# One ring tile and one ScalarE eviction a tick for O^T and dQ^T in a two-block attention backward

## The chip, the cores and the metric

The kernel runs on one core of one Trainium2 chip. The metric is the device time of one execution in microseconds (us). Engines: TensorE (PE) multiplies, PEld is its weight load, VectorE (DVE), ScalarE (ACT) and GpSimd (POOL) do the rest of the arithmetic, and SyncE (SP) issues DMAs. TensorE writes to PSUM, which has eight banks. SBUF holds everything else.

## The reference: what is computed

Two independent blocks, A and B, each an attention with cached keys and values and its full backward pass. The output of the forward pass and ten gradients are returned, in bf16.

```
B, Sq, D = 8, 96, 640
H, Sk, Dh = 32, 512, 128
q = (x @ wq).reshape(B, Sq, H, Dh).transpose(0, 2, 1, 3)
scores = einsum("bhqd,bhkd->bhqk", q, k_cache) * (Dh ** -0.5)
p = softmax(scores, axis=-1)
o = einsum("bhqk,bhkd->bhqd", p, v_cache)
out = o.transpose(0, 2, 1, 3).reshape(B, Sq, H * Dh) @ wo
...
out0 = concatenate([out_A, out_B], axis=-1)
grads = vjp of all ten inputs at grad_out
```

For one head and batch element (96 query rows, 512 keys) the backward needs dV = P^T dO, dP = dO V^T, dS = P * (dP - delta) with delta the row sums of O * dO, dK = dS^T Q and dQ = dS K. Then dwo = O^T g and dwq = x^T dQ per head, and dx = dQ wq^T summed over the heads. The factor Dh ** -0.5 belongs once to Q (and through it to dK) and once to dQ.

## The kernel before

Work is cut into **ticks**: one tick for each pair of head and batch element, 32 x 8 for each block, 512 in all. The kernel writes its steps into a list (`Emitter`) with a tick and a slot; the list is sorted and run, and a tile scheduler then orders instructions on each engine and inserts the waits. One pair's work is spread over several ticks (`OFF`): S and softmax at +3 (`c_s2a`, `c_s2b`, `c_s3a`, `c_s3b`), P^T and dV at +4, O^T at +5, dP and dS at +6, dS^T and dK at +7, dQ^T at +8. So one tick works on six pairs at different stages.

Within a tick TensorE does, in this order: S; if needed the transposes of K (`c_s1`); dQ^T and the four transposes of dS (`c_s78`, lines 412 and 419); dK (436); O^T and the four transposes of P (`c_s45`, lines 342 and 349); dV (366); dP (394) and delta (396); then work of whole heads: transposes of wo and wq (`pB`), projections of Q and dO (`pC`), natural-order copies (`pD`, `qA`), dwo (`qB`), dwq (`qD`), and the group sums for out and dx (`gU`, line 515).

All results leave PSUM through the 8 banks of one pool (`bank`). Two tiles a tick matter here:

- `optp_ps` (line 332): O^T of one pair in the first 96 fp32 columns, P^T of another behind it. ScalarE evicts both, L352 into `OT_h`, L355 into `PT_sb`.
- `dq_dst_ps` (line 404): dQ^T of one pair in the first 96 fp32 columns, dS^T of another behind it. DVE copies dS^T to `dST_sb` (L421), and ScalarE evicts dQ^T into `dQT_h` with the factor `scale` (L425).

ScalarE otherwise carries the exponential (L307), the evictions of dV (L369) and dK (L439), and some of the heads' evictions (`evac`, L155). DVE carries the row maximum (L297), the reciprocal (L317), dS (L398), copies and sums. POOL scales P (L326), forms `prod` = O^T * dO^T for delta (L384) and issues the stores. The DMA queue of SP brings K and V, and transposes V always and K in half of the ticks.

`OT_h` and `dQT_h` are tiles of one head each, [128, 768] bf16, eight buffers each, from the pool `hst` (lines 218 and 219). They are read by `prod` (OT_h), by the transposes of `qA` (L459) and by `gU`, which adds up to six heads at a time. `gU` evicts the first group to fp32 accumulators, adds later ones on DVE (L517), and writes the last with L535 and L537.

Of the kernel before, what the change touches and what calls it, by code (L numbers as in the profile page):

```python
# [15 lines left out]
class Emitter:  # L16
# [4 lines left out]
    def add(self, tick, slot, fn):  # L21
        self.items.append((tick, slot, self.n, fn))
        self.n += 1
# [21 lines left out]
OFF = dict(ldk=-5, ldv=-3, kt=-3, vt=0, s2=3, s3=3, s4=4, s5=5, s6=6, s7=7, s8=8)  # L45
# [8 lines left out]
def build_block(tc, em, tick0, blk, x, kc, vc, wq, wo, g_all, out_all, dx, dk, dv, dwq, dwo, ident, ones, pools, HG=6, first=True, groups=None):  # L54
    nc = tc.nc
# [3 lines left out]
    T = B * Sq  # L59
# [38 lines left out]
    def bank(shape, dt, name):  # L98
        return ps.tile(shape, dt, name=name, tag="bank")
# [3 lines left out]
    SB = {}  # L103
    HS = pools["HS"]
    CS = pools["CS"]

    stp = pools["stp"]

# [94 lines left out]
    def pB(h):  # L203
        def f():
            st = HS[(blk, h)]
            woT_ps = bank([128, DC * 128], BF16, "woT_ps")
            for c in range(DC):
                nc.tensor.transpose(woT_ps[:, c * 128:(c + 1) * 128], st["wo_h"][:, c * 128:(c + 1) * 128], ident[:])
            woT_h = hd.tile([128, DC * 128], BF16, name="woT_h", bufs=1)
            evac(EV["pB0"], woT_h[:], woT_ps[:])  # L210
            st["woT_h"] = woT_h
            wqT_ps = bank([128, DC * 128], BF16, "wqT_ps")
            for c in range(DC):
                nc.tensor.transpose(wqT_ps[:, c * 128:(c + 1) * 128], st["wq_h"][:, c, :], ident[:])
            wqT_h = hst.tile([128, D], BF16, name="wqT_h")
            evac(EV["pB1"], wqT_h[:], wqT_ps[:])
            st["wqT_h"] = wqT_h
            st["OT_h"] = hst.tile([128, T], BF16, name="OT_h")
            st["dQT_h"] = hst.tile([128, T], BF16, name="dQT_h")
            st["QT_h"] = hd.tile([128, T], BF16, name="QT_h")  # L220
            st["dOT_h"] = hd.tile([128, T], BF16, name="dOT_h")
        return f
# [104 lines left out]
                st["P_sb"] = P_sb  # L327
        return f

    def c_s45(k5, k4, k6):  # L330
        def f():
            pt_ps = bank([128, 1024], BF16, "optp_ps")
            ot_view = None
            if False:
                pass
            if k5 is not None:
                st = CS[(k5[0], k5[1], k5[2])]
                hs = HS[(k5[0], k5[1])]
                tok = slice(k5[2] * Sq, (k5[2] + 1) * Sq)
# [3 lines left out]
                ot_view = (OT_ps, hs, tok)  # L343
            if k4 is not None:
                st4 = CS[(k4[0], k4[1], k4[2])]
                P_sb = st4["P_sb"]
                PT_ps = pt_ps[:, 256:256 + KC * Sq]
                for c in range(KC):
                    nc.tensor.transpose(PT_ps[:, c * Sq:(c + 1) * Sq], P_sb[:, c * 128:(c + 1) * 128], ident[0:Sq, 0:Sq])  # L349
            if ot_view is not None:  # L350
                OT_ps, hs, tok = ot_view
                nc.scalar.activation(hs["OT_h"][:, tok], OT_ps, ACT.Identity, scale=1.0)  # L352
            if k4 is not None:
                PT_sb = wk.tile([128, KC * Sq], BF16, name="PT_sb", bufs=3)
                nc.scalar.activation(PT_sb[:], PT_ps, ACT.Identity, scale=1.0)  # L355
                st4["PT_sb"] = PT_sb
        return f
# [30 lines left out]
    def c_s6(h, b):  # L388
        def f():
# [7 lines left out]
            dS_sb = wk.tile([Sq, Sk], BF16, name="dS_sb", bufs=3)  # L397
            nc.vector.scalar_tensor_tensor(dS_sb[:], dP_ps[:], dl_ps[:, 0:1], st["P_sb"][:], op0=ALU.subtract, op1=ALU.mult)  # L398
            st["dS_sb"] = dS_sb
        return f  # L400

    def c_s78(k8, k7):
        def f():
            x_ps = bank([128, 1024], BF16, "dq_dst_ps")
            dq_view = None
            if k8 is not None:
                st = CS[(k8[0], k8[1], k8[2])]
                hs = HS[(k8[0], k8[1])]
                tok = slice(k8[2] * Sq, (k8[2] + 1) * Sq)
                dQT_ps = x_ps[:, 0:2 * Sq].bitcast(F32)  # L410
                for c in range(KC):
                    nc.tensor.matmul(dQT_ps, st["K_sb"][:, c, :], st["dST_sb"][:, c * Sq:(c + 1) * Sq], start=(c == 0), stop=(c == KC - 1))  # L412
                dq_view = (dQT_ps, hs, tok)
            if k7 is not None:
                st7 = CS[(k7[0], k7[1], k7[2])]
                dS_sb = st7["dS_sb"]
                dST_ps = x_ps[:, 256:256 + KC * Sq]
                for c in range(KC):
                    nc.tensor.transpose(dST_ps[:, c * Sq:(c + 1) * Sq], dS_sb[:, c * 128:(c + 1) * 128], ident[0:Sq, 0:Sq])  # L419
                dST_sb = wk.tile([128, KC * Sq], BF16, name="dST_sb", bufs=3)  # L420
                nc.vector.tensor_copy(dST_sb[:], dST_ps)  # L421
                st7["dST_sb"] = dST_sb
            if dq_view is not None:
                dQT_ps, hs, tok = dq_view
                nc.scalar.activation(hs["dQT_h"][:, tok], dQT_ps, ACT.Identity, scale=scale)  # L425
                del CS[(k8[0], k8[1], k8[2])]
        return f

    def c_s7(h, b):
# [51 lines left out]
    def qD(h, c_lo, c_hi):  # L481
        def f():
# [8 lines left out]
            for ci in range(ncn):  # L491
                c = c_lo + ci
                for t in range(TT):
                    nc.tensor.matmul(w_ps[:, ci * 256:(ci + 1) * 256], S["x_nat"][:, t, c * 128:(c + 1) * 128], dQnat[:, t].rearrange("p a d -> p (a d)"),  # L494
                                     start=(t == 0), stop=(t == TT - 1))
            evac(EV["qD"], dwq_sb[:, c_lo:c_hi, :].rearrange("p a b -> p (a b)"), w_ps[:, 0:ncn * 256])
            st["dwq_n"] += ncn
            if st["dwq_n"] == DC:
                with nc.allow_non_contiguous_dma(reason="dwq slice of two heads"):
# [5 lines left out]
    def gU(g, which, t, gi):  # L505
        def f():
            acc = S.get("out_acc" if which == 0 else "dx_acc")
            dst_flat = out_flat if which == 0 else dx_flat
            (c0, w) = gsplits[gi]
            o_ps = bank([128, w], F32, "o_ps")  # L510
            for hh in range(groups[g]):
# [3 lines left out]
                nc.tensor.matmul(o_ps[:], src[:, t * 128:(t + 1) * 128], rhs, start=(hh == 0), stop=(hh == groups[g] - 1))  # L515
            if 0 < g < NG - 1:
                nc.vector.tensor_tensor(acc[:, t, c0:c0 + w], o_ps[:], acc[:, t, c0:c0 + w], op=ALU.add)  # L517
                return
            if g == 0 and NG > 1:
                evac(EV["gU"], acc[:, t, c0:c0 + w], o_ps[:])  # L520
                return
            end = not first and which == 1
            if end:
# [3 lines left out]
                    S["ob"] = stp.tile([128, D], BF16, name="ob", tag="stage")  # L527
                ob = S["ob"][:]
            if NG == 1:
                evac(EV["gU"], ob[:, c0:c0 + w], o_ps[:])  # L530
            else:
                if end and t in (0, 2):
                    tmp = S["xT"][:].rearrange("p c k -> p (c k)").bitcast(F32)[:, (t // 2) * D + c0:(t // 2) * D + c0 + w]
                    nc.scalar.activation(tmp, o_ps[:], ACT.Identity, scale=1.0)
                    nc.gpsimd.tensor_tensor(ob[:, c0:c0 + w], tmp, acc[:, t, c0:c0 + w], op=ALU.add)  # L535
                else:
                    nc.vector.tensor_tensor(ob[:, c0:c0 + w], o_ps[:], acc[:, t, c0:c0 + w], op=ALU.add)  # L537
# [6 lines left out]
    def k_on_pe(h, b):  # L544
        return (b // NB) % 2 == 0

    S45 = pools["S45"]
    S78 = pools["S78"]
    for g in range(NG):
        h0 = GH0[g]  # L550
        for hh in range(groups[g]):
# [12 lines left out]
            for b in range(B):  # L564
# [18 lines left out]
                S45.setdefault(ct + OFF["s5"], [None, None, None])[0] = (blk, h, b)  # L583
                S45.setdefault(ct + OFF["s4"], [None, None, None])[1] = (blk, h, b)
                S45.setdefault(ct + OFF["s6"], [None, None, None])[2] = (blk, h, b)
                S78.setdefault(ct + OFF["s8"], [None, None])[0] = (blk, h, b)
                S78.setdefault(ct + OFF["s7"], [None, None])[1] = (blk, h, b)
# [26 lines left out]
    pools["c_s78"] = c_s78  # L614
    return tick0 + H * B


def _kernel_impl(tc, A_x, A_k_cache, A_v_cache, A_wq, A_wo, B_x, B_k_cache, B_v_cache, B_wq, B_wo, grad_out,
# [13 lines left out]
    with ExitStack() as ctx:  # L632
# [21 lines left out]
        pools["S45"] = {}  # L654
        pools["S78"] = {}
        pools["HS"] = {}
        pools["CS"] = {}
        em = Emitter()
# [1 line left out]
        for blk, args in enumerate(((A_x, A_k_cache, A_v_cache, A_wq, A_wo, grad_out, out_0, out_1, out_2, out_3, out_4, out_5),  # L660
# [7 lines left out]
        for tk, (k5, k4, k6) in pools["S45"].items():  # L668
            em.add(tk, SLOTS["S5"], pools["c_s45"](k5, k4, k6))
        for tk, (k8, k7) in pools["S78"].items():  # L670
            em.add(tk, SLOTS["S8"], pools["c_s78"](k8, k7))
        em.run()


# [62 lines left out]
```

## Time and profile before

| | |
|---|---|
| Median of 4 runs | 1736.52 us (1720.19 to 1747.04) |
| Profiled execution | 1734.96 us |
| Span of its trace | 1733.2 us, granted TensorE clock 0.997 |
| Busy share PE, PEld | 97%, 78% |
| Busy share ACT, DVE, POOL | 81%, 77%, 61% |
| Instructions on ACT, DVE, POOL | 4027, 3040, 1747 |
| DMA | 424.69 MB, mean 245 GB/s |

A row of instruction groups reads: line, engine, operation, output<-inputs, shapes and count, then total busy us and mean ns of one, then the engine's idle time just before them and what ended it. A row of waits reads: engine and what it wanted to do, what it waited for, total us, number of times, longest us. A row of the chain reads: start in us, length in us, what. The chain is followed back from the last instruction of the program to what released each step. A busy time includes an instruction's tail, in which the next one is already under way.

### The profile page before, as it was taken

To read this page: it belongs to the slowest core of one execution; us is meant where nothing else is said; L and a number is where in the kernel's file an instruction comes from. 1 tells how busy PE (TensorE), PEld (TensorE's weight loads), DVE (VectorE), ACT (ScalarE), POOL (GpSimd) and SP (SyncE) were. 2 spreads that over 40 slices of the span, in tenths; PEclk is the share of its full clock that TensorE was granted. 3 is DMA by queue.
4 is the path that set the end of the run, shared out by engine and by line. 5 is a ranking of instruction groups with operands and counts; after the bars stand their busy time and mean duration, and the time that the engine had idled before them with its cause. 6 is when DMAs were issued, how large, how long until landed. Compare 5 with 4: busy or idle time off the path is not lost.

```text
span 1733.2 us, 57521 instructions
## 1 busy us (share of the span) xinstructions
PE 1681.3 (97%) x21811; PEld 1346.0 (78%) x21976; DVE 1328.5 (77%) x3040; ACT 1411.6 (81%) x4027; POOL 1049.6 (61%) x1747
## 2 busy tenths in 40 slices
PE   8999999999999999999897999999999999999998
PEld 7877778878778777778676777887788778778876
DVE  6876678778878877778776876787788778777877
ACT  7988789779779878878766997997799779868974
POOL 4666466556657656656555764665566557646654
PEclk9999999999999999999998999999999999999999
DMA  9999999989999989999999999999999999989983
GB/s 276 268 247 269 239 238 270 256 214 249 264 208 256 279 202 227 263 253 262 267 235 208 267 275 240 243 266 246 221 251 284 228 214 263 267 216 245 271 223 131
DMA packets 606774, 424.69 MB, mean 245 GB/s; under 512 B 425696, under 2 KB 564320, under 8 KB 606496
## 3 DMA queue, kind: packets, MB, share of 16 engines
q1 hardware_dynamic: 552912, 243.65, 70.7%
q0 software_dynamic: 53584, 177.35, 31.7%
q8 instruction: 172, 2.82, 0.7%
q14 instruction: 106, 0.87, 0.2%
HBM read 161.09 MB, written 159.12 MB: 185 GB/s over the span
## 4 chain that ended last, share of the span: by engine, by line
PE 82%; ACT 8%; DMA 4%; issue 3%; DVE 2%; POOL 1%; SPq 0%; ACTq 0%; DVEq 0%; POOLq 0%
PE o_ps L515 11%; PE q_ps L240 11%; PE S_ps L295 6%; PE dwq_ps L494 6%; PE dK_ps L436 5%; PE dP_ps L394 5%; PE dwo_ps L474 5%; PE dV_ps L366 5%; PE dq_dst_ps L419 4%; PE dq_dst_ps L412 4%; PE optp_ps L349 4%; PE optp_ps L342 4%; ACT E_sb L307 3%; PE n_ps L255 3%; PE kT_ps L282 3%
## 5 line engine op out<-in xcount | busy, mean ns | idle before, releaser
L326 POOL TENSOR_SCALAR P_sb<-E_sb,rinv 96x512 bf16<-96x512 bf16 x512 | 353.4, 690 | 387.0 <-DVE rinv L317 377.6
L307 ACT ACTIVATE E_sb<-S_ps,negm 96x512 bf16<-96x512 f32 x512 | 355.5, 694 | 206.2 <-DVE negm L297 181.5
L398 DVE SCALAR_TENSOR_TENSOR dS_sb<-dP_ps,dl_ps,P_sb 96x512 bf16<-96x512 f32 x512 | 382.8, 748 | 73.9 <-PE dl_ps L396 54.7
L297 DVE TENSOR_REDUCE negm<-S_ps 96x1 f32<-96x512 f32 x512 | 348.1, 680 | 62.5 <-PE S_ps L295 58.1
L439 ACT ACTIVATE dK_sb<-dK_ps 128x512 bf16<-128x512 f32 x512 | 308.5, 603 | 64.2 <-PE dK_ps L436 60.6
L369 ACT ACTIVATE dV_sb<-dV_ps 128x512 bf16<-128x512 f32 x512 | 319.9, 625 | 0.0
L375 POOL DMA_DIRECT2D out_dram<-dV_sb x256 | 194.1, 758 | 148.2 <-ACT dV_sb L369 129.0
L355 ACT ACTIVATE PT_sb<-optp_ps 128x384 bf16<-128x384 bf16 x512 | 261.2, 510 | 1.1 <-PE optp_ps L349 1.1
L375 POOL DMA_DIRECT2D out_dram<-dK_sb x256 | 193.0, 754 | 84.0 <-ACT dK_sb L439 48.7
L394 PE MATMUL dP_ps<-VT,dOT_h 128*96 128x512 bf16 x512 | 195.3, 381 | 10.4 <-DMA VT<-V_sb 9.5
L366 PE MATMUL dV_ps<-dOnat_h,P_sb 96*128 96x128 bf16 x2048 | 198.1, 219 | 1.0 <-DVE dOnat_h L158 0.8
L436 PE MATMUL dK_ps<-Qnat_h,dS_sb 96*128 96x128 bf16 x2048 | 198.1, 219 | 0.0
L384 POOL TENSOR_TENSOR prod<-OT_h,dOT_h 128x96 bf16<-128x96 bf16 x512 | 186.9, 365 | 8.6 <-ACT OT_h L352 4.3
L421 DVE COPY dST_sb<-dq_dst_ps 128x384 bf16<-128x384 bf16 x512 | 177.4, 346 | 11.7 <-PE dq_dst_ps L419 11.3
L349 PE MATMUL optp_ps<-ident,P_sb 96*128 96x96 bf16 x2048 | 172.1, 205 | 2.8 <-POOL P_sb L326 2.4
L419 PE MATMUL dq_dst_ps<-ident,dS_sb 96*128 96x96 bf16 x2048 | 172.4, 206 | 1.2 <-DVE dS_sb L398 1.2
L342 PE MATMUL optp_ps<-PT_sb,V_sb 128*128 128x96 bf16 x2048 | 172.3, 206 | 0.0
L317 DVE RECIPROCAL rinv<-rowsum 96x1 f32<-96x1 f32 x512 | 79.5, 155 | 120.0 <-ACT E_sb L307 113.2
L412 PE MATMUL dq_dst_ps<-dST_sb,K_sb 128*128 128x96 bf16 x2048 | 170.8, 206 | 0.6 <-DVE dS_sb L398 0.2
L412 PEld LDWEIGHTS <-K_sb 128*128 128x128 bf16 x2048 | 131.8, 98 | 23.4 <-issue 1.0
L240 PE MATMUL q_ps<-gT,woT_h 128*128 128x256 bf16 (+1 forms) x622 | 136.5, 325 | 1.6 <-ACT gT L155 0.6
L474 PE MATMUL dwo_ps<-g_nat,Onat 128*128 128x320 bf16 x768 | 135.4, 298 | 1.2 <-ACT E_sb L307 0.2
(87 smaller groups left out, 3822.2 us busy)
## 6 DMA issues: line engine op xcount, KB each, us to landing
out_dram<-dV_sb POOLq DMA_DIRECT2D x256, 256.0 KB, 4.8
out_dram<-dK_sb POOLq DMA_DIRECT2D x256, 256.0 KB, 4.9
K_sb<-in_A_k_cache_dram SPq DMA_DIRECT2D x128, 256.0 KB, 5.0
V_sb<-in_A_v_cache_dram SPq DMA_DIRECT2D x128, 256.0 KB, 4.9
K_sb<-in_B_k_cache_dram SPq DMA_DIRECT2D x128, 256.0 KB, 4.7
V_sb<-in_B_v_cache_dram SPq DMA_DIRECT2D x128, 256.0 KB, 4.9
out_dram<-dwo_sb POOLq DMA_DIRECT2D x63, 160.0 KB, 4.4
out_dram<-dwq_sb POOLq DMA_DIRECT2D x31, 320.0 KB, 5.9
```

The source lines that it names most:

```text
L240: nc.tensor.matmul(q_ps[:], lhs(c), rhsT[:, c, t0:t0 + w], start=(c == 0), stop=(c == DC - 1))
L297: nc.vector.tensor_reduce(negm[:], S_ps[:], axis=AX.X, op=ALU.max, negate=True)
L307: nc.scalar.activation(E_sb[:], st["S_ps"][:], ACT.Exp, bias=st["negm"][:], scale=1.0, accum_out=rowsum[:])
L326: pinned(nc.gpsimd.tensor_scalar(P_sb[:], st["E_sb"][:], st["rinv"][:], 0.0, op0=ALU.mult, op1=ALU.add))
L366: nc.tensor.matmul(dV_ps[:, c * 128:(c + 1) * 128], P_sb[:, c * 128:(c + 1) * 128], hs["dOnat_h"][:, b * 128:(b + 1) * 128], start=True, s ...
L369: nc.scalar.activation(SB[(blk, h, b // 2, "v")][:, b % 2], dV_ps[:], ACT.Identity, scale=1.0)
L375: nc.gpsimd.dma_start(dst[b - 1:b + 1, h].rearrange("b (p c) d -> p b (c d)", c=KC), SB.pop((blk, h, b // 2, which))[:])
L394: nc.tensor.matmul(dP_ps[:], hs["dOT_h"][:, tok], st["VT"], start=True, stop=True)
L398: nc.vector.scalar_tensor_tensor(dS_sb[:], dP_ps[:], dl_ps[:, 0:1], st["P_sb"][:], op0=ALU.subtract, op1=ALU.mult)
L412: nc.tensor.matmul(dQT_ps, st["K_sb"][:, c, :], st["dST_sb"][:, c * Sq:(c + 1) * Sq], start=(c == 0), stop=(c == KC - 1))
L436: nc.tensor.matmul(dK_ps[:, c * 128:(c + 1) * 128], dS_sb[:, c * 128:(c + 1) * 128], hs["Qnat_h"][:, b * 128:(b + 1) * 128], start=True, s ...
L439: nc.scalar.activation(SB[(blk, h, b // 2, "k")][:, b % 2], dK_ps[:], ACT.Identity, scale=1.0)
```

## The change

`OT_h` and `dQT_h` of all heads move into one tile `OD` of [128, 2, 8, 768] bf16, a ring with a slot for each head. Its size is that of the sixteen buffers that it replaces. The two PSUM tiles are divided in another way. `x_ps` now holds O^T and dQ^T next to each other (96 fp32 columns each) and P^T behind them; `dst_ps` holds dS^T alone. `c_s78` becomes `c_s8`, at the same slot; it allocates `x_ps`, computes dQ^T into it, and does dS^T in the other bank. `c_s45`, later in the same tick, takes the same `x_ps`, adds O^T and P^T, and ends with one ScalarE activation that reads 192 columns and writes both 96-column strips into `OD` by an access pattern of two steps. Only the first and last three ticks have one of the two strips. Since one instruction has one factor, the factor `scale` of dQ^T moves to its users: to the eviction of dwq, and to the evictions and adds of dx (the plain adds of dx become multiply-adds).

```diff
+            st["slot"] = (blk * H + h) % OD.shape[2]
+            st["OT_h"] = OD[:, 0, st["slot"]]
+            st["dQT_h"] = OD[:, 1, st["slot"]]
...
+    def c_s8(tick, k8, k7):
+        def f():
+            XP[tick] = bank([128, 1024], BF16, "x_ps")
+            if k8 is not None:
+                st = CS[(k8[0], k8[1], k8[2])]
+                dQT_ps = XP[tick][:, 2 * Sq:4 * Sq].bitcast(F32)
+                for c in range(KC):
+                    nc.tensor.matmul(dQT_ps, st["K_sb"][:, c, :], st["dST_sb"][:, c * Sq:(c + 1) * Sq], start=(c == 0), stop=(c == KC - 1))
...
+            if k7 is not None:
+                st7 = CS[(k7[0], k7[1], k7[2])]
+                dST_ps = bank([128, KC * Sq], BF16, "dst_ps")
+                for c in range(KC):
+                    nc.tensor.transpose(dST_ps[:, c * Sq:(c + 1) * Sq], st7["dS_sb"][:, c * 128:(c + 1) * 128], ident[0:Sq, 0:Sq])
+                dST_sb = wk.tile([128, KC * Sq], BF16, name="dST_sb", bufs=3)
+                nc.vector.tensor_copy(dST_sb[:], dST_ps[:])
...
+    def c_s45(tick, k8, k5, k4):
+        def f():
+            pt_ps = XP.pop(tick)
...
-                PT_ps = pt_ps[:, 256:256 + KC * Sq]
+                PT_ps = pt_ps[:, 4 * Sq:4 * Sq + KC * Sq]
...
-                nc.scalar.activation(hs["OT_h"][:, tok], OT_ps, ACT.Identity, scale=1.0)
+            both = [(k, which) for which, k in enumerate((k5, k8)) if k is not None]
+            if both:
+                at = [(HS[(k[0], k[1])]["slot"], k[2] * Sq) for k, _ in both]
+                v = OD[:, both[0][1], at[0][0], at[0][1]:at[0][1] + Sq]
+                src = pt_ps[:, 2 * Sq * both[0][1]:2 * Sq * (both[-1][1] + 1)].bitcast(F32)
+                if len(both) == 2:
+                    step = (OD.shape[2] + at[1][0] - at[0][0]) * T + at[1][1] - at[0][1]
+                    v = bass.AP(v.tensor, v.offset, [v.ap[0], (step, 2), (1, Sq)])
+                    src = src.rearrange("p (a q) -> p a q", a=2)
+                nc.scalar.activation(v, src, ACT.Identity, scale=1.0)
...
-                nc.scalar.activation(hs["dQT_h"][:, tok], dQT_ps, ACT.Identity, scale=scale)
...
-            evac(EV["qD"], dwq_sb[:, c_lo:c_hi, :].rearrange("p a b -> p (a b)"), w_ps[:, 0:ncn * 256])
+            evac(EV["qD"], dwq_sb[:, c_lo:c_hi, :].rearrange("p a b -> p (a b)"), w_ps[:, 0:ncn * 256], scale)
...
+            def add(dst):
+                if which == 0:
+                    nc.vector.tensor_tensor(dst, o_ps[:], acc[:, t, c0:c0 + w], op=ALU.add)
+                else:
+                    nc.vector.scalar_tensor_tensor(dst, o_ps[:], scale, acc[:, t, c0:c0 + w], op0=ALU.mult, op1=ALU.add)
```

More of the change, by code (lines that the diff above doesn't have):

```diff
@@ L105, in build_block @@
     CS = pools["CS"]
+    XP = pools["XP"]
+    OD = pools["OD"]
     stp = pools["stp"]
@@ L217, in f @@
             st["wqT_h"] = wqT_h
-            st["OT_h"] = hst.tile([128, T], BF16, name="OT_h")
-            st["dQT_h"] = hst.tile([128, T], BF16, name="dQT_h")
+            st["slot"] = (blk * H + h) % OD.shape[2]
+            st["OT_h"] = OD[:, 0, st["slot"]]
+            st["dQT_h"] = OD[:, 1, st["slot"]]
             st["QT_h"] = hd.tile([128, T], BF16, name="QT_h")
@@ L328, in c_s3b @@
         return f
-    def c_s45(k5, k4, k6):
+    def c_s8(tick, k8, k7):
         def f():
[L332 to L335, printed above, removed]
+            XP[tick] = bank([128, 1024], BF16, "x_ps")
[4 more added lines that the diff above has]
+                    nc.tensor.matmul(dQT_ps, st["K_sb"][:, c, :], st["dST_sb"][:, c * Sq:(c + 1) * Sq], start=(c == 0), stop=(c == KC - 1))
+                del CS[(k8[0], k8[1], k8[2])]
+            if k7 is not None:
[5 more added lines that the diff above has]
+                nc.vector.tensor_copy(dST_sb[:], dST_ps[:])
+                st7["dST_sb"] = dST_sb
+        return f
+    def c_s45(tick, k8, k5, k4):
+        def f():
+            pt_ps = XP.pop(tick)
             if k5 is not None:
                 st = CS[(k5[0], k5[1], k5[2])]
-                hs = HS[(k5[0], k5[1])]
-                tok = slice(k5[2] * Sq, (k5[2] + 1) * Sq)
                 OT_ps = pt_ps[:, 0:2 * Sq].bitcast(F32)
@@ L342, in f @@
                     nc.tensor.matmul(OT_ps, st["V_sb"][:, c, :], st["PT_sb"][:, c * Sq:(c + 1) * Sq], start=(c == 0), stop=(c == KC - 1))
-                ot_view = (OT_ps, hs, tok)
             if k4 is not None:
@@ L346, in f @@
                 P_sb = st4["P_sb"]
-                PT_ps = pt_ps[:, 256:256 + KC * Sq]
+                PT_ps = pt_ps[:, 4 * Sq:4 * Sq + KC * Sq]
                 for c in range(KC):
                     nc.tensor.transpose(PT_ps[:, c * Sq:(c + 1) * Sq], P_sb[:, c * 128:(c + 1) * 128], ident[0:Sq, 0:Sq])
-            if ot_view is not None:
-                OT_ps, hs, tok = ot_view
-                nc.scalar.activation(hs["OT_h"][:, tok], OT_ps, ACT.Identity, scale=1.0)
+            both = [(k, which) for which, k in enumerate((k5, k8)) if k is not None]
[8 more added lines that the diff above has]
+                nc.scalar.activation(v, src, ACT.Identity, scale=1.0)
             if k4 is not None:
@@ L399, in f @@
             st["dS_sb"] = dS_sb
[L400 to L426, printed above, removed]
         return f
@@ L510, in f @@
             o_ps = bank([128, w], F32, "o_ps")
+            sc = scale if which == 1 else None
             for hh in range(groups[g]):
@@ L515, in f @@
                 nc.tensor.matmul(o_ps[:], src[:, t * 128:(t + 1) * 128], rhs, start=(hh == 0), stop=(hh == groups[g] - 1))
+            def add(dst):
[3 more added lines that the diff above has]
+                    nc.vector.scalar_tensor_tensor(dst, o_ps[:], scale, acc[:, t, c0:c0 + w], op0=ALU.mult, op1=ALU.add)
             if 0 < g < NG - 1:
-                nc.vector.tensor_tensor(acc[:, t, c0:c0 + w], o_ps[:], acc[:, t, c0:c0 + w], op=ALU.add)
+                add(acc[:, t, c0:c0 + w])
                 return
             if g == 0 and NG > 1:
-                evac(EV["gU"], acc[:, t, c0:c0 + w], o_ps[:])
+                evac(EV["gU"], acc[:, t, c0:c0 + w], o_ps[:], sc)
                 return
@@ L529, in f @@
             if NG == 1:
-                evac(EV["gU"], ob[:, c0:c0 + w], o_ps[:])
+                evac(EV["gU"], ob[:, c0:c0 + w], o_ps[:], sc)
             else:
@@ L533, in f @@
                     tmp = S["xT"][:].rearrange("p c k -> p (c k)").bitcast(F32)[:, (t // 2) * D + c0:(t // 2) * D + c0 + w]
-                    nc.scalar.activation(tmp, o_ps[:], ACT.Identity, scale=1.0)
+                    nc.scalar.activation(tmp, o_ps[:], ACT.Identity, scale=scale)
                     nc.gpsimd.tensor_tensor(ob[:, c0:c0 + w], tmp, acc[:, t, c0:c0 + w], op=ALU.add)
                 else:
-                    nc.vector.tensor_tensor(ob[:, c0:c0 + w], o_ps[:], acc[:, t, c0:c0 + w], op=ALU.add)
+                    add(ob[:, c0:c0 + w])
             if gi == len(gsplits) - 1:
@@ L545, in k_on_pe @@
         return (b // NB) % 2 == 0
-    S45 = pools["S45"]
-    S78 = pools["S78"]
+    SX = pools["SX"]
     for g in range(NG):
@@ L582, in build_block @@
                 em.add(ct + OFF["s4"], SLOTS["S4"], c_s4(h, b))
[L583 to L587, printed above, removed]
+                for i, o in enumerate(("s8", "s7", "s5", "s4")):
+                    SX.setdefault(ct + OFF[o], [None] * 4)[i] = (blk, h, b)
                 em.add(ct + OFF["s6"], SLOTS["S6"], c_s6(h, b))
@@ L613, in build_block @@
     pools["c_s45"] = c_s45
-    pools["c_s78"] = c_s78
+    pools["c_s8"] = c_s8
     return tick0 + H * B
@@ L653, in _kernel_impl @@
             nc.tensor.matmul(warm_ps[:], warm[:], warm[:], start=True, stop=True)
-        pools["S45"] = {}
-        pools["S78"] = {}
+        pools["SX"] = {}
+        pools["XP"] = {}
+        pools["OD"] = pools["const"].tile([128, 2, HG + 2, A_x.shape[0] * A_x.shape[1]], BF16, name="OD", bufs=1)
         pools["HS"] = {}
@@ L667, in _kernel_impl @@
             t_next = build_block(tc, em, t_next, blk, *args, ident, ones, pools, HG=HG, first=(blk == 0), groups=grps)
[L668 to L671, printed above, removed]
+        for tk, (k8, k7, k5, k4) in pools["SX"].items():
+            em.add(tk, SLOTS["S8"], pools["c_s8"](tk, k8, k7))
+            em.add(tk, SLOTS["S5"], pools["c_s45"](tk, k8, k5, k4))
         em.run()
```

## The prediction

> **What bounds the kernel now.** I read the page from the top: busy time, the chain that ended last, the groups; then the list of waits, the chain between 797 and 804 us, and the timeline of ScalarE in the same place.
>
> ```profile
> PE 1681.3 (97%) x21811; PEld 1346.0 (78%) x21976; DVE 1328.5 (77%) x3040; ACT 1411.6 (81%) x4027; POOL 1049.6 (61%) x1747
> ...
> PE 82%; ACT 8%; DMA 4%; issue 3%; DVE 2%; POOL 1%; SPq 0%; ACTq 0%; DVEq 0%; POOLq 0%
> ```
>
> TensorE is busy 97% of the span and carries 82% of the chain. It is not quite full, since a matmul's busy time includes its tail: in the timeline four 96-column matmuls follow each other every 42 ns though each shows 206 ns, and 512 columns take 215 ns to the next start, not 379. I set each matmul's start against its predecessor's start and streaming time. What is left over, without the places where a record is missing, is about 83 us of gaps: some 27 us end with a DMA (start, change of block, a few late K^T and V^T), 20 us with DVE or POOL (P 7.9, dS 4.9, Qnat 3.2), 31 us with an instruction of ScalarE, most of which gave a PSUM bank free, and the rest with none. Only the last two kinds can respond to this change, so 51 us is all there is to win.
>
> The groups that the change touches, by form:
>
> ```profile
> L355 ACT ACTIVATE PT_sb<-optp_ps 128x384 bf16<-128x384 bf16 x512 | 261.2, 510 | 1.1 <-PE optp_ps L349 1.1
> L421 DVE COPY dST_sb<-dq_dst_ps 128x384 bf16<-128x384 bf16 x512 | 177.4, 346 | 11.7 <-PE dq_dst_ps L419 11.3
> L352 ACT ACTIVATE OT_h<-optp_ps 128x96 bf16<-128x96 f32 x512 | 134.4, 262 | 0.5 <-PE optp_ps L349 0.5
> L425 ACT ACTIVATE dQT_h<-dq_dst_ps 128x96 bf16<-128x96 f32 x512 | 133.1, 260 | 2.1 <-PE dq_dst_ps L412 2.1
> ```
>
> The two small activations have almost no idle time before them: ScalarE has a backlog when it reaches them. Where the backlog is longest the chain leaves TensorE and runs along ScalarE for some microseconds:
>
> ```profile
> 800.15 0.79 ACT E_sb L307 x2
> 800.94 0.14 ACT dQT_h L425
> 801.08 0.48 ACT dK_sb L439
> 801.56 0.14 ACT OT_h L352
> 801.70 0.38 ACT PT_sb L355
> 802.08 0.37 ACT dV_sb L369
> ```
>
> This is the tick in which a head's wo and wq are transposed: little for TensorE, one more eviction of 0.76 us for ScalarE. Some 48 of 512 ticks look like this, mostly two in a row at a head's change.
>
> And the waits that say who is not pressed:
>
> ```profile
> POOL P_sb L326 <- DVE rinv L317: 377.6, 346, 10.9
> ACT E_sb L307 <- DVE negm L297: 181.5, 196, 3.9
> DVE dS_sb L398 <- PE dl_ps L396: 54.7, 153, 6.4
> DVE dx_acc L517 <- PE o_ps L515: 31.7, 42, 1.9
> ```
>
> In the other ticks ScalarE waits for the row maximum, that is, for TensorE's own pace; time saved on it there is worth nothing.
>
> **The two evictions become one.** By busy time each tick loses 262 + 260 ns and gains one activation of 192 columns. Rows of the timeline (start, duration) give its price:
>
> ```profile
> 801.41 0.29 ACT L352 ACTIVATE OT_h<-optp_ps 128x96 bf16<-128x96 f32 x1
> 801.54 0.54 ACT L355 ACTIVATE PT_sb<-optp_ps 128x384 bf16<-128x384 bf16 x1
> 801.91 0.65 ACT L369 ACTIVATE dV_sb<-dV_ps 128x512 bf16<-128x512 f32 x1
> 802.39 0.76 ACT L155 ACTIVATE woT_h<-woT_ps 128x640 bf16<-128x640 bf16 x1
> ```
>
> From start to next start it is 131 ns in the median for 96 columns, 371 for 384 and 478 for 512, so 0.833 ns a column and 51 ns an instruction. The combined one takes 131 + 96 x 0.833 = 211 ns where the two took 262: 51 ns less a tick, 26 us of ScalarE's time over 509 full ticks. The busy column will fall more, by 262 + 260 - 342 = 180 ns a tick, some 92 us, since one tail goes too; that is no time. The Trainium skill ("ScalarE: Activation LUTs", what ACT_TABLE_LOAD costs) puts an activation with immediates at 186 ns plus 0.833 ns a column, 93 ns of it overlapped by the next: by that a merged pair saves 93 ns a tick, 47 us. The slope agrees; the fixed part in this trace is 51 ns, and I use that. Of the saving only the 48 ticks on the chain count: 48 x 51 ns = 2.4 us. The output of two distant strips of 96 columns has no row; I take no surcharge, as every row with a split output fits the same line (bounds: 0 to 50 ns, the latter undoing the saving).
>
> **A wait that goes.** L421 on DVE and L425 on ScalarE read one bank, so all dQT evictions but one wait for DVE's copy of dST (the built program names it 511 times). It ends nothing in the list of waits, because the copy ended a median 0.70 us before the eviction did. Removing it is worth nothing by itself. No wait is added: the combined activation waits for P^T's transposes on TensorE, as L352 did, and behind it stand PT_sb and dV_sb as before.
>
> **Banks.** Here is most of what I expect. Before, dq_dst_ps was held from the first dQ matmul until ScalarE got to L425, a mean 2.02 us a tick; optp_ps from O to PT_sb, 1.89 us; together 3.91 us. After, x_ps is held from dQ (0.58 us ahead of O) to PT_sb, 1.89 + 0.58 = 2.47 us, and dst_ps from the transposes of dS to DVE's copy, 1.14 us: 3.61 us. The skill speaks against the first half: "PSUM — Partial Sum Buffer", in its summary of rules for kernel authors, asks that a bank be evacuated promptly, and dQ's result now waits 0.45 us longer in its bank. By that rule alone the edit costs; by the sum of both banks it gives 0.30 us a tick back, because the dS half no longer waits for ScalarE.
>
> The built order settles who then waits for whom. TensorE's order is the same but for 22 ticks in which O goes ahead of the dS transposes (cost 0 to 22 x 0.17 = 3.7 us; I take 0, DVE waits for that copy's input only 11.3 us in all). With each bank wait of the changed program laid on the times of this trace, none falls below its old margin, and several grow: S from the DMA-transposed K starts 51 ns after its bank came free in a quarter of its ticks or more, and would have 161 ns at the tenth percentile and 438 at the quarter. Summing, gap by gap, what the later margin could take away: S 9.6 us (7.4 with K^T by DMA, 2.2 with K^T by TensorE), dP behind woT_h 3.8, q_ps 3.7, dQ 1.6, the others 2.0: 20.7 us. Ends: 0, if the next wait (P from POOL) takes over at once, and 20.7 and more, if S being earlier brings maximum, exponential and P earlier too. I take 18, near the upper end, as S heads the row of steps that ends in P.
>
> **Later O.** O^T reaches SBUF 80 ns later after its matmuls. prod on POOL waits for it, dl for prod. TensorE waits for prod under 1 us in all, and the dl matmul has 113 ns of margin even at its first percentile; POOL idles 377.6 us ahead of the P step behind it. Cost 0; 512 x 80 ns = 41 us if that cover were gone. dQ^T is up to a microsecond later, but read first one or two ticks (3.4 us each) on.
>
> **The scale.** dwq's eviction becomes a multiply, 64 of 512 and 32 of 256 columns; the dx adds get a factor, 58 of each width. The nearest row with a factor is dS at 748 ns against 690 for the plain add of 512: at most 60 ns x 212 = 13 us of DVE, at least 0. DVE is idle 29.4 us ahead of the dwq evictions and 31.6 ahead of the dx adds; I count 0. Where ScalarE evicts dx it already had a factor operand of 1.0.
>
> **Sum.** 2.4 + 18 = about 20 us. The profiled execution was 1734.96 us (span 1733.2 and 1.8 around it), 1.6 under the median of the runs, 1736.5: forecast 1715. The four runs spread over 1.5%, so about 2% is what a measurement here can tell from no change: under 1702 or over 1771.
>
> **Rivals.** First, the backlog collapses. ScalarE's runs feed on themselves: a late E makes P late, late P makes dV and PT late. If slack in the banks lets TensorE run ahead through the heavy ticks, all 31 us behind ScalarE go and half of the 20 us behind P and dS: 41 us, 1694. For it: these gaps lie in the same ticks. Against: the load of a heavy tick falls only 51 ns of some 2.8 us.
>
> Second, hidden. The gaps move to P, or TensorE arrives sooner at K^T and V^T, whose queues show a DMA share of 1.0 and more in most 100 us windows. Then only about 5 us stay: 1731.
>
> Third, slower. x_ps, one bank of eight, is held 0.58 us longer than optp_ps was, and this decides where TensorE needs a bank while dst_ps is still waiting for a DVE that is behind. An eighth of it every tick is 72 ns, x 512 = 37 us: 1773. It decides from the point at which the two banks together are held over the old 3.91 us. Against it: dST's copy would have to come 0.30 us later in the mean.
>
> That the change doesn't do what it says is excluded: ScalarE has 3,008 instructions where it had 3,517.
>
> **How the numbers follow.** Forecast 50%, 1715, own range 1700 to 1726, about 12 of the 50 below 1702. Collapse 23%, 1694. Hidden 13%, 1731. Slower 14%, of which 3 inside 2%. Faster 12 + 23 = 35%, same 38 + 13 + 3 = 54%, slower 11%. The range from 1688 to 1750 leaves out the slow case and about 5 of the collapse.
>
> **What would show it.** The combined eviction near 340 ns and 211 ns to the next start; ScalarE's busy time near 1320 us; fewer E, dK and woT releases ahead of S and dP; ScalarE's share of the chain under 8%; P's wait on TensorE no greater. I am wrong if the combined form takes over 400 ns, if DVE's copy of dST comes later, or if TensorE's gaps stay near 83 us with new names.

## The result, and the profile after

The changed kernel takes 1716.6 us in the median (44 runs, 1705.2 to 1732.3). With more runs the kernel before has a median of 1726.7 us (63 runs, 1712.9 to 1750.8). The ratio is 0.9951, with a 95% interval from 0.9937 to 0.9966: 6 to 11 us faster. All ratios here compare fast executions alone, those within 1.5% of the fastest of their kernel, so they differ a little from quotients of the medians. The mean granted TensorE clock is 0.9960 over the 44 runs; over the 93 later runs of the kernel before it lies between 0.9953 and 0.9967 by session, so the gain is not one of clock. The change is real and inside the 2% that the prediction called hard to tell. The forecast of 1715 is met. The forecast gain is not: 20 us were expected from the profiled execution (1734.96 us), which lay 8 us over what later proved to be the median. The profiled execution after is 1715.65 us, just under its median.

Busy time and the chain of the changed kernel, from its page, to be set beside the first lines of the prediction:

```profile
PE 1669.2 (97%) x21811; PEld 1342.1 (78%) x21976; DVE 1322.7 (77%) x3040; ACT 1383.2 (81%) x3518; POOL 1046.7 (61%) x1747
...
PE 88%; DMA 5%; ACT 2%; issue 2%; POOL 1%; DVE 1%; SPq 0%; DVEq 0%; POOLq 0%; ACTq 0%
```

ScalarE's share of the chain went from 8% to 2%, while its busy share of the span stays at 81%. The average told nothing of what the change was worth; the chain showed where to look.

The groups of the changed kernel that answer to the four shown before, with the adds that took over the scale and the plain add beside them:

```profile
L378 ACT ACTIVATE PT_sb<-x_ps 128x384 bf16<-128x384 bf16 x512 | 257.3, 502 | 1.1 <-PE x_ps L365 1.1
L348 DVE COPY dST_sb<-dst_ps 128x384 bf16<-128x384 bf16 x512 | 177.2, 346 | 10.1 <-PE dst_ps L346 9.0
L375 ACT ACTIVATE OD<-x_ps 128x192 bf16<-128x192 f32 x509 | 170.6, 335 | 0.7 <-PE x_ps L365 0.5
L162 DVE TENSOR_SCALAR dwq_sb<-dwq_ps 128x512 bf16<-128x512 f32 x64 | 44.0, 687 | 29.4 <-PE dwq_ps L490 29.4
L518 DVE SCALAR_TENSOR_TENSOR dx_acc<-o_ps,dx_acc 128x512 f32<-128x512 f32 x48 | 33.2, 691 | 31.3 <-PE o_ps L512 31.1
L516 DVE TENSOR_TENSOR out_acc<-o_ps,out_acc 128x512 f32<-128x512 f32 x48 | 33.1, 690 | 28.0 <-PE o_ps L512 25.2 <-PE q_ps L243 1.9 <-PE S_ps L298 0.7
```

The combined eviction takes 335 ns. The multiply-add takes 691 ns against 690 for the plain add, and the scaled eviction of dwq 687 against 688 before: here the scale costs DVE nothing.

ScalarE's timeline in a tick of the kind in which it fell behind before (start, duration):

```profile
792.02 0.75 ACT L157 ACTIVATE woT_h<-woT_ps 128x640 bf16<-128x640 bf16 x1
792.60 0.74 ACT L310 ACTIVATE E_sb<-S_ps,negm 96x512 bf16<-96x512 f32 x1
...
793.26 0.65 ACT L435 ACTIVATE dK_sb<-dK_ps 128x512 bf16<-128x512 f32 x1
793.74 0.39 ACT L375 ACTIVATE OD<-x_ps 128x192 bf16<-128x192 f32 x1
793.95 0.56 ACT L378 ACTIVATE PT_sb<-x_ps 128x384 bf16<-128x384 bf16 x1
```

From OD's start to PT_sb's is 0.21 us. The chain of waits in the same place:

```profile
792.60 0.22 PE dV_ps L389 x4
792.83 0.22 PE dP_ps L417
793.05 0.00 PE dl_ps L419
793.05 0.24 PE q_ps L243
793.29 0.22 PE S_ps L298
793.50 0.05 issue
793.56 0.81 PE q_ps L243 x3
```

Before, the chain ran along ScalarE through such a tick; here it stays with TensorE, while ScalarE is just as busy. Waits that grew, first of the kernel before, then after:

```profile
PEld L295 <- DMA KT<-K_sb: 10.6, 6, 3.1
...
PEld L349 <- POOL P_sb L326: 4.1, 9, 1.3
```

```profile
PEld L298 <- DMA KT<-K_sb: 14.1, 8, 4.5
...
PEld L365 <- POOL P_sb L329: 8.1, 27, 1.4
```

TensorE now waits for P more than it did; in a second profile of the changed kernel that line reads 8.5 us, so this repeats. The wait for a transposed K doesn't: there it is 8.0 us, less than before.

### The profile page after: what moved, and what is told of

Same layout as the page of the kernel before. It is cut to its first block, busy times and chain, and to the rows that moved or that the text cites. A ratio compares the mean times of both kernels' runs of the same rounds, so it can differ in the third digit from the quotient of the medians.

```text
span 1713.9 us, 57116 instructions
## 1 busy us (share of the span) xinstructions
PE 1669.2 (97%) x21811; PEld 1342.1 (78%) x21976; DVE 1322.7 (77%) x3040; ACT 1383.2 (81%) x3518; POOL 1046.7 (61%) x1747
## 4 chain that ended last, share of the span: by engine, by line
PE 88%; DMA 5%; ACT 2%; issue 2%; POOL 1%; DVE 1%; SPq 0%; DVEq 0%; POOLq 0%; ACTq 0%
PE o_ps L512 11%; PE q_ps L243 11%; PE S_ps L298 6%; PE dK_ps L432 6%; PE dV_ps L389 6%; PE dP_ps L417 6%; PE dwo_ps L470 6%; PE dwq_ps L490 6%; PE x_ps L365 5%; PE x_ps L340 5%; PE dst_ps L346 5%; PE x_ps L359 5%; PE n_ps L258 3%; PE kT_ps L285 3%; PE nat_ps L455 3%; DMA KT<-K_sb 2%
## 5 line engine op out<-in xcount | busy, mean ns | idle before, releaser
L392 ACT ACTIVATE dV_sb<-dV_ps 128x512 bf16<-128x512 f32 x512 | 315.8, 617 | 0.0
L378 ACT ACTIVATE PT_sb<-x_ps 128x384 bf16<-128x384 bf16 x512 | 257.3, 502 | 1.1 <-PE x_ps L365 1.1
L512 PEld LDWEIGHTS <-OD 128*128 128x128 bf16 x1536 | 132.2, 98 | 99.7 <-issue 0.2
L407 POOL TENSOR_TENSOR prod<-OD,dOT_h 128x96 bf16<-128x96 bf16 x512 | 186.0, 363 | 9.6 <-ACT OD L375 5.6
L348 DVE COPY dST_sb<-dst_ps 128x384 bf16<-128x384 bf16 x512 | 177.2, 346 | 10.1 <-PE dst_ps L346 9.0
L365 PE MATMUL x_ps<-ident,P_sb 96*128 96x96 bf16 x2048 | 172.4, 206 | 4.2 <-POOL P_sb L329 3.0
L375 ACT ACTIVATE OD<-x_ps 128x192 bf16<-128x192 f32 (+1 forms) x515 | 172.0, 334 | 4.6 <-PE x_ps L340 3.8
L359 PE MATMUL x_ps<-PT_sb,V_sb 128*128 128x96 bf16 x2048 | 172.5, 206 | 0.6 <-ACT PT_sb L378 0.4
L346 PE MATMUL dst_ps<-ident,dS_sb 96*128 96x96 bf16 x2048 | 172.4, 206 | 0.5 <-DVE dS_sb L421 0.5
L340 PE MATMUL x_ps<-dST_sb,K_sb 128*128 128x96 bf16 x2048 | 171.0, 206 | 0.5 <-ACT PT_sb L378 0.4
```

The costliest lines, as they stand in the source:

```text
L392: nc.scalar.activation(SB[(blk, h, b // 2, "v")][:, b % 2], dV_ps[:], ACT.Identity, scale=1.0)
```

## TensorE's gaps, one table for all kernels

As in the prediction, each matmul's start was set against its predecessor's start plus its streaming time, leaving out places with a missing record, and each remaining gap was given to the instruction or DMA that the matmul waited for last. In us, of one profiled execution each:

| kernel | DMA | ScalarE | DVE | POOL | none | sum | profiled time | time less sum |
|---|---|---|---|---|---|---|---|---|
| before | 27.6 | 31.1 | 12.1 | 8.3 | 4.3 | 83.4 | 1735.0 | 1651.6 |
| after | 25.3 | 10.7 | 13.9 | 10.9 | 5.7 | 66.5 | 1715.7 | 1649.2 |
| after, once more | 24.2 | 11.0 | 14.1 | 11.0 | 4.6 | 64.9 | 1715.6 | 1650.7 |
| two evictions | 28.5 | 15.4 | 10.4 | 20.3 | 6.6 | 81.2 | 1731.1 | 1649.9 |
| two evictions, order held | 25.5 | 18.9 | 9.6 | 12.9 | 5.4 | 72.3 | 1724.1 | 1651.8 |
| before, dS^T in its own bank | 31.7 | 29.4 | 11.3 | 5.9 | 6.4 | 84.7 | 1734.7 | 1650.0 |
| before, scale moved | 20.1 | 29.8 | 12.2 | 8.1 | 6.0 | 76.2 | 1726.1 | 1649.9 |
| after, 7 banks | 18.8 | 80.2 | 9.1 | 6.7 | 3.9 | 118.7 | 1767.3 | 1648.6 |
| before, 7 banks | 10.1 | 113.6 | 8.9 | 3.1 | 2.6 | 138.3 | 1787.0 | 1648.7 |
| after, rinv late | 21.4 | 10.4 | 13.4 | 17.9 | 4.1 | 67.2 | 1715.9 | 1648.7 |

The last column stays within 1648.6 to 1651.8 us over 71 us of difference in time. (The two kernels with an added activation, below, leave 1648 and 1654.) So the sum of gaps accounts for the time of these executions, and about 1650 us is what TensorE's own stream takes. Not every profiled execution is a typical one of its kernel. With rinv late, 1715.9 us was the fastest of twelve (median 1721.1), and with dS^T in its own bank 1734.7 the slowest of twelve (median 1725.1); with the scale moved it lay 5.7 us over the median. What repeats best is the sum without DMA: 55.8 us before and 56.1 with the scale moved, 41.2 and 40.7 in the two profiles of the changed kernel.

## The experiments

The theory after the result was the prediction's own: nearly all of the gain comes from the banks (**bank theory**). The rival was that it comes from ScalarE's 51 ns a tick (**ScalarE theory**).

**The changed kernel once more.**

> The changed kernel once more, beside the three that take it apart. Both theories expect the ratio to the kernel before of the first result, 0.995 (0.993 to 0.997), and a trace in which ScalarE ends about 11 us of TensorE's gaps where it ended 31 us before.

Measured 0.994 (0.9895 to 0.9985), ScalarE's gaps 11.0 us. It repeats.

**The banks without the merge.** From the changed kernel:

```diff
-                nc.scalar.activation(v, src, ACT.Identity, scale=1.0)
+                for k, which in both:
+                    v = OD[:, which, HS[(k[0], k[1])]["slot"], k[2] * Sq:(k[2] + 1) * Sq]
+                    nc.scalar.activation(v, pt_ps[:, 2 * Sq * which:2 * Sq * (which + 1)].bitcast(F32), ACT.Identity, scale=1.0)
```

> The changed kernel with its banks and its scale, but O^T and dQ^T evicted by two activations of 96 columns again. Bank theory (nearly all of the gain is that dS^T's bank comes free without ScalarE): it keeps nine tenths of the gain, ratio 0.9955 (0.994 to 0.998), ScalarE's share of TensorE's gaps near 13 us. ScalarE theory (the gain is the 51 ns a tick): it is back at the kernel before, 0.999 to 1.001, and the gaps behind ScalarE near 30 us.

Measured 1.0024 (0.9987 to 1.0062). By time this is what the ScalarE theory said. By gaps it is not: those behind ScalarE fell to 15.4 us, near the bank theory's 13, and those behind POOL rose to 20.3 us:

```profile
PEld L365 <- POOL P_sb L329: 15.5, 38, 1.8
...
PE x_ps L365 <- POOL P_sb L329: 8.8, 15, 1.7
```

The built orders show a second difference that the edit brought along. In 21 ticks the scheduler had put dS (0.65 us) ahead of the reciprocal on DVE, and P waits for the reciprocal. (The traces show a third: in 12 ticks ScalarE evicts Q^T behind the exponential instead of ahead of it.) Two more kernels take that apart.

**The same with DVE's order held.** dS is emitted behind the reciprocal in those 21 ticks, by an edge that orders the two and makes neither wait for the other to end:

```diff
+LATE = [16, 32, 48, 80, 96, 128, 160, 176, 208, 240, 256, 288, 304, 336, 352, 384, 400, 432, 448, 480, 496]
...
+                if (blk * H + h) * B + b in LATE:
+                    ctx.enter_context(tc.issue_after(CS[(blk, h, b + 3)]["rinv_ins"].ins))
+                nc.vector.scalar_tensor_tensor(dS_sb[:], dP_ps[:], dl_ps[:, 0:1], st["P_sb"][:], op0=ALU.subtract, op1=ALU.mult)
```

> The first split kernel again (banks and scale of the change, two evictions), now with DVE's order held to that of the changed kernel: in 21 ticks the scheduler had put dS ahead of the reciprocal there. Order theory (those 21 ticks cost the split kernel 21 x 0.65 us = up to 14 us through a late P): most of the loss against the changed kernel goes, ratio to before 0.996 to 0.999, TensorE's gaps behind P back from 20 to about 11 us. ScalarE theory (52 ns a tick cost the loss themselves): it stays at 1.001 to 1.004.

Measured 0.9953 (0.9917 to 0.9989), gaps behind P back at 12.9 us:

```profile
PEld L368 <- POOL P_sb L332: 8.3, 28, 1.3
...
PE x_ps L368 <- POOL P_sb L332: 2.9, 4, 1.2
```

So with two evictions and DVE's order that of the changed kernel, the divided banks and the moved scale are faster than the kernel before without the merge. The ScalarE theory, which put this kernel at 1.001 or more, falls as an account of the whole gain. How much the merge adds on top is not resolved by time, since the intervals of 0.9953 and 0.9951 overlap. The profiles don't give nearly all to the banks either. ScalarE's gaps are 18.9 us without the merge and 10.7 with it: 12 us of the fall come with the banks, 8 with the merge. Of all gaps but those behind DMA (55.8 us before, 46.8 here, 41.2 after) it is 9 and 6. And ScalarE's share of the chain, 8% before and 2% after, is 7% here:

```profile
PE 82%; ACT 7%; DMA 5%; issue 3%; DVE 2%; POOL 1%; SPq 0%; ACTq 0%; DVEq 0%; POOLq 0%
```

**The order alone.** The changed kernel with dS ahead of the reciprocal in the same 21 ticks:

```diff
+LATE = [19, 35, 51, 83, 99, 131, 163, 179, 211, 243, 259, 291, 307, 339, 355, 387, 403, 435, 451, 483, 499]
...
+                    if (blk * H + h) * B + b in LATE:
+                        ctx.enter_context(tc.issue_after(CS[(blk, h, b - 3)]["dS_ins"].ins))
+                    nc.vector.reciprocal(rinv[:], st["rowsum"][:])
```

> The changed kernel with DVE's order alone changed, to that of the first split kernel: in 21 ticks dS goes ahead of the reciprocal. Order theory: 6 to 14 us slower than the changed kernel, ratio to before 0.998 to 1.003, and the gaps behind P at 18 to 22 us. ScalarE theory: no cost, 0.994 to 0.996.

Measured 0.9956 (0.9922 to 0.999): not resolved from the changed kernel, and below the 0.998 of the order theory, though its interval reaches that. The gaps behind POOL rose to 17.9 us (the theory had 18 to 22), but the sum of gaps was 67.2, near the 66.5 and 64.9 of the changed kernel, because this execution, the fastest of twelve, had 3 to 4 us less behind DMA. Without DMA the gaps are 45.8 us, some 5 more than in the changed kernel; with two evictions the same order had added 6 (52.7 against 46.8). So by gaps the order costs about the same in both, and the 0.7% between the two split kernels is more than it accounts for. Holding DVE's order there also put ScalarE's 12 evictions of Q^T and 20 of POOL's stores back in place; ScalarE's order was not tried alone, so how much of that loss is DVE's order is open.

**dS^T in a bank of its own, nothing else.** From the kernel before:

```diff
-                dST_ps = x_ps[:, 256:256 + KC * Sq]
+                dST_ps = bank([128, KC * Sq], BF16, "dst_ps")
```

> The kernel before with one edit: dS^T in a bank of its own, three tiles a tick (O with P^T, dQ^T, dS^T), two evictions, scale where it was. Bank theory: the gain is there without the merge, ratio 0.995 (0.992 to 0.998); if three tiles a tick are too many for eight banks, 1.00 or above. ScalarE theory: 1.000 (0.998 to 1.002), as ScalarE does the same work.

Measured 0.9975 (0.9942 to 1.0009), which separates neither theory. The profile does say something: gaps behind ScalarE stay at 29.4 us under new names (dP behind the exponential and dQ behind PT_sb, about 5.0 each). A reading that fits, and is not shown, is that dS^T's bank comes free early, but a third tile a tick takes it up again. The gain would then need both halves: dS^T apart from what ScalarE reads, and dQ^T in a bank that is held anyway. The order of evictions on ScalarE changed along with this edit and wasn't held.

**The scale alone.** From the kernel before, the factor moved to dwq and dx and nothing else.

```diff
-                nc.scalar.activation(hs["dQT_h"][:, tok], dQT_ps, ACT.Identity, scale=scale)
+                nc.scalar.activation(hs["dQT_h"][:, tok], dQT_ps, ACT.Identity, scale=1.0)
```

> The kernel before with the scale of dQ moved alone, to dwq's evictions and the dx adds. Both theories: 1.000 (0.999 to 1.001), the multiply-adds at 690 to 750 ns and the scaled evictions of dwq at 690 ns, all in DVE's idle time. If DVE's extra time were on the path: up to 13 us, 1.007.

Measured 0.9964 (0.9932 to 0.9996), a little faster where nothing was expected. Orders on all engines are those of the kernel before, and no group of 50 or more instructions changed its mean duration by more than 4 ns. Its gaps behind ScalarE, DVE and POOL (29.8, 12.2, 8.1) are those of the kernel before as well; only those behind DMA are lower, 20.1 for 27.6. Its twelve executions also had a higher granted clock, 0.9972 in the mean against 0.9959 for the kernel before in the same session; as the last section shows, a lower clock goes with late DMAs, and 0.0013 of it with some 4 us, against the 6 us measured. The upper end is so near to 1 that it may be chance. It stays open, and with it whether part of the gain in time goes with the scale; hardly any of the fall of ScalarE's gaps does.

**One bank fewer.** Both kernels with seven banks:

```diff
-            ps=P(name="ps", bufs=8, space=PSUM),
+            ps=P(name="ps", bufs=7, space=PSUM),
```

> The changed kernel with seven PSUM banks in its pool in place of eight. Bank theory: banks are what ScalarE's backlog is passed on through, so one of eight less costs clearly, ratio to the kernel before 1.00 to 1.03, with the gaps behind ScalarE back at 25 us or more. ScalarE theory: banks are not what is short, 0.995 to 0.998.

> The kernel before with seven PSUM banks. Bank theory: it loses more than the changed kernel does by the same cut, since its two tiles hold 0.30 us a tick more: 1.02 to 1.05. ScalarE theory: 1.000 to 1.005.

Measured 1.0192 (1.0153 to 1.0232) for the changed kernel, against its own 0.9951 a loss of 2.4%; and 1.0366 (1.0325 to 1.0407) for the kernel before, 3.7%. The chains, changed kernel first:

```profile
PE 69%; ACT 14%; issue 6%; DVE 6%; DMA 4%; POOL 1%; ACTq 0%; SPq 0%; DVEq 0%; POOLq 0%
```

```profile
PE 65%; ACT 17%; DVE 8%; issue 7%; DMA 2%; POOL 1%; ACTq 0%; SPq 0%; DVEq 0%; POOLq 0%
```

This is the clearest support that banks are what ScalarE's backlog is passed on through. With a bank less ScalarE's gaps rise to 80 and 114 us, though ScalarE has the same instructions. With eight banks the changed kernel is ahead by 0.5%, with seven by 1.7% (1.0192 / 1.0366 = 0.983). The pair doesn't share this lead out: the divided banks and the merged eviction both give banks back sooner.

**The price of ScalarE's time.** The changed kernel with an added activation a tick, of 96 columns and then, with the order held, of one column:

```diff
+                extra = wk.tile([128, 1], BF16, name="extra", bufs=2)
+                nc.scalar.activation(extra[:], pt_ps[:, 2 * Sq * both[0][1]:2 * Sq * both[0][1] + 2].bitcast(F32), ACT.Identity, scale=1.0)
```

> The changed kernel with a second activation of 96 columns a tick, which copies O^T once more to a tile that nothing reads: 131 ns of ScalarE more a tick. It prices ScalarE's time. Bank theory: 131 ns count on some 20 to 50 ticks alone, 3 to 7 us, ratio 0.997 to 0.999. ScalarE theory: if 51 ns a tick brought 8 us, 131 ns cost 20 us, 1.007.

> The changed kernel, order held, with one more activation of a single column a tick, some 52 ns, the fixed cost that the merge removed. If ScalarE's time costs what 131 ns cost before (15 us, 0.23 of each ns), 6 us: ratio 0.997 to 1.000. By the 48 ticks of the prediction alone, 2.5 us: 0.996. Equal to the split kernel with the same order, as both add the same time.

Measured 1.004 (1.0008 to 1.0072) for 131 ns, and 1.0041 (1.0007 to 1.0075) for 51 ns. At one price for each ns the second should have cost 0.4 of the first: what was added is hardly time alone. In the first, ScalarE's gaps are 32.6 us. In the second they are 20.0, much as with two evictions (18.9), and 41.8 us lie behind DMA:

```profile
PE dP_ps L422 <- DMA VT<-V_sb: 15.3, 7, 4.4
...
PEld L422 <- DMA VT<-V_sb: 6.9, 3, 2.9
```

This execution is 8 us over its kernel's median and has the lowest granted clock of all the profiled ones, 0.991. But the other eleven share in it: the mean clock is 0.9936 in this kernel against 0.9953 for the kernel before in its session, and 0.9949 against 0.9967 in the first. Why the V transposes are late wasn't tried; the extra tile also takes room in SBUF, so that what lies behind it may have moved. As a price of ScalarE's time this pair is inconclusive; the kernel with two evictions and the order held is the better measure.

**Two tries to go further.**

```diff
-EV = dict(pB0="act", ...
+EV = dict(pB0="dve", ...
```

> The changed kernel with the eviction of the transposed wo, 64 times 0.72 us, moved from ScalarE to DVE: 580 ns of ScalarE less in just the ticks in which it falls behind. Both theories: what ScalarE still ends of TensorE's gaps (11 us) shrinks to 5 to 8 us; DVE takes 400 ns more in a tick in which the row maximum and dS are due, which costs up to as much. 0.992 to 0.998.

> The changed kernel with the reciprocal ahead of dS on DVE in the 56 ticks in which the scheduler has it behind. If a late P is what bounds the changed kernel, the 4.5 us of gaps that P ends in these ticks shrink: 0.992 to 0.995. If the exponential is late there anyway, dS and what follows it come later for nothing: 0.996 to 1.005.

Measured 0.9947 (0.9916 to 0.9978) with woT on DVE and 0.9946 (0.9912 to 0.998) with the reciprocal first in 56 ticks: neither can be told from the changed kernel. The first did not lower ScalarE's gaps (14.8 us for 10.7), against its expectation. The second raised those behind P to 19.5 us instead of lowering them; what makes P late there was not looked for further. Neither is a better version.

## Why the prediction was right or wrong

**The bound and the 83 us of gaps: right.** The table shows that gaps account for the time of each execution in it to about 3 us. (The 51 us that could respond are those behind ScalarE, DVE and POOL; gaps with no releaser are not counted in it.)

**The two evictions become one: right in its size, wrong in the busy column.** Start to next start is 211 ns in the median, as worked out from the rows. Two of 131 against one of 211 is 51; by the fixed part in the Trainium skill ("ScalarE: Activation LUTs", what ACT_TABLE_LOAD costs) it would have been 93. The duration is 335 ns for 342. No surcharge for the two strips appeared. ScalarE's busy time fell by 28.4 us (1411.6 to 1383.2), not by 92. I had summed tails, but the column counts the time in which the engine is busy, so tails that overlap are counted once, and it fell by about the 26 us of real time.

**Where the 51 ns count: undervalued.** I counted them on 48 ticks, 2.4 us. The split kernel with order held has 8 us more gaps behind ScalarE than the changed one. So the merge seems to act in more places than the chain of the kernel before showed; its net effect on time isn't resolved.

**Banks: the bank times right, the size right only together with the merge.** x_ps is held 2.46 us (predicted 2.47), dst_ps 1.15 us (1.14). Gaps behind ScalarE fell by 20.4 us, from 31.1 to 10.7; the sum gap by gap had given 20.7. That they agree is in part luck. The 20.7 were meant for the banks alone; with two evictions the banks took 12 us away, and the other 8 came with the merge, for which the prediction had 2.4. The Trainium skill's "Evacuate promptly" ("PSUM — Partial Sum Buffer", summary of rules for kernel authors) taken alone speaks for a loss, since dQ's result waits longer; the runs show a gain, as the sum over both banks had it. That banks are short the seven-bank pair bears out.

**The step that failed is "I take 18, near the upper end".** It let almost all of the 20.7 us through, because an earlier S should bring P earlier. P came no earlier: gaps behind POOL rose from 8.3 to 10.9 us and those behind DVE from 12.1 to 13.9. Measured, some 8.5 us of 20 arrive (0.0049 x 1726.7). The rival called "hidden" has some share in that. The profiles before and after don't show how much directly, because the profiled execution before was itself 8.3 us over its median. Against the kernel with the scale alone moved, which has the same banks and order and was profiled at 1726.1 us, an ordinary time for the kernel before, though over its own median, the account is: ScalarE 29.8 to 10.7, POOL +2.8, DVE +1.7, DMA +5.2 (20.1 to 25.3), none -0.3; in all 9.7 us less. I had set the 27 us behind DMA aside as unable to respond. They may respond, and in the wrong direction: in the table they are 10 us in the slowest kernel here, 19 in the next and 20 to 32 in those between 1716 and 1735 us. Among the latter they follow no order, so part of it is variation between executions, and the DMA share of what was given back is argued, not shown. What does repeat: the gaps not behind DMA fell by 15 us in each pairing, about 4 of the 20 going to P and to DVE's steps, while the time fell by 6 to 11. Where the rest went is open.

**The four-run median.** I set the sum against an execution of 1734.96 us and a median of 1736.5; 63 runs give 1726.7. The forecast time is near by luck: an anchor 8 us too high met a gain 10 us too large by the medians, 12 by the ratio. It would have been 1707 from the right anchor, inside the range still.

**Later O, scale, wait that goes: priced at nothing, and no cost was seen.** POOL's wait for O^T is 5.6 us after and 4.3 before; the adds are unchanged at 691 and 690 ns. **The slower rival** needed dST's copy to come 0.30 us later; the dS half of the bank time moved by 0.01 us. **The collapse** did not come: ScalarE's gaps fell to 11, not to none, and those behind P rose.

## What to carry to other kernels

Before a change of PSUM tiles, add up how long all tiles of a step are held, and ask which engine lets each go: dq_dst_ps, read by two engines, came free only after the later one, 0.70 us behind the first in the median. A gap that is removed is not yet time; name the next wait of the same instruction and give it a share: of 20 us behind ScalarE, 6 to 11 arrived here. And when an experiment changes an instruction's length, compare the scheduled order of all engines before reading its time: here 21 swapped pairs on DVE and 12 on ScalarE came along unasked.

## What the runs showed of the hardware that was not expected

An added activation of one column, 51 ns a tick, cost as much as one of 96 columns, 131 ns a tick (1.0041 and 1.0040 of the kernel before, against 0.995 without), the shorter one with 41.8 us of gaps behind DMA. Its cause was not found.

A long wait for a DMA mostly costs more than its gap, since a stretch of half the granted clock goes with it. In the kernel before TensorE waits 6 us for one transposed V, up to 934 us, and stretches of its profile show (busy time and number of instructions of PE, PEld, DVE, ACT and POOL, then the granted clock, the DMA share and GB/s):

```profile
928.00:932.00 4.00, 0.10 (x2) 0.01 (x1) 0.16 (x1) 1.95 (x7) 2.54 (x4) 0.98 1.03 212
932.00:942.00 10.00, 5.15 (x36) 3.68 (x36) 2.29 (x5) 1.80 (x6) 0.54 (x1) 0.50 1.16 195
942.00:946.00 4.00, 4.00 (x67) 3.71 (x66) 3.40 (x8) 3.07 (x10) 1.66 (x4) 0.99 1.20 213
```

The 14 traces have 40 such stretches, of 3.4, 6.8 or 10.2 us, besides one at the end of each. All 40 begin during a wait of TensorE for a DMA of 1.65 us or more, or within 7 us of its end; 14 of the 52 waits over 2 us have none. The kernel with one added column has seven, 31 us in all, where the changed kernel has two with 14. Over 269 executions the time goes with the clock, 3.2 us for each 0.001 (correlation -0.85 within kernel and session), and half of the clock for 3.4 us is 0.001 of the span. So much of the spread between executions of one kernel goes with late DMAs and the clock that follows them, and a mean clock beside each ratio tells whether two kernels met the same share of them.
